# Third matrix product entirely by seven half products, with the order of all later instructions written anew

## The chip, the cores and the metric

One core of a Trainium2 chip runs the whole kernel. The metric is the device time of one execution in microseconds; a comparison uses the median over several runs. The profiled execution has a time of its own, given beside its span.

## The reference

Causal attention over q, k, v (2 batches, 12 heads, 448 rows, 64 per head), then a gated layer, then a hard-swish layer, all in float32:

```python
x = attention(q, k, v)                              # 896 x 768
x = ((1 / (1 + exp(-(x @ w_gate)))) * (x @ w_val)) @ w_out    # 768 -> 1536 -> 768
h = x @ w2_in                                       # 768 -> 2048
g = h * clip(h + 3, 0, 6) / 6
out = g @ w2_out                                    # 2048 -> 768
```

The weights come as float64 words and are turned into float32 on the chip.

## The kernel before

**Numbers.** Each factor is split into a high and a low part (`hi`, `lo`, both fp32r), and each product is three matrix products: hi·hi, hi·lo, lo·hi (`TERMS`). A split is either a ScalarE copy and a VectorE subtraction (`split`, `decode_b`), or two ScalarE copies (hi, and the negated source into lo) and a transfer on POOL's queue that adds the source to lo (`dma_split`, L186).

**Units.** The weights are cut into units of 128 x 768. A unit is loaded by SP into one of three `raw` slots, and decoded by one ScalarE scaling (`scale`) and four VectorE operations (`shift`, `clamp`, `join`, `sign`; `decode_a`, L208). `w_dec` (L699) decodes the next unit of the stream and loads the one three places on, which may start when the `sign` of the slot's old unit is through; `w_parts` (L710) splits units that are used plainly.

**Products.** Behind attention there are four matrix products: first (x with w_gate and w_val, units g0.. and v0..), second (with w_out, units o0.0.., giving y), third (y with w2_in, 16 units i0 to i15), last (with w2_out). All but the last have 448 columns in a matrix instruction, the two halves (b = 0, 1) of the 896 rows. A *plain block* (`halves`, L234) is 36 instructions for one unit: 6 slices, 3 terms, 2 halves. A *pair* (class `Pairs`, L718) does two units together by Strassen's way with seven half products P1 to P7 of 9 instructions each, 63 in all. It needs sums and differences of the pair's weights (`w_sums`: four VectorE operations into S) split into factors g1 to g4, of the moving side the four forms T1 to T4 beside three plain blocks of it (B11, B21, B22), and additions of the products (the copies C11, C12, C22 by ScalarE, `add`s by VectorE).

**Order of a pair run** (`run`, L845): P1, P2 of pair p, P4 of pair p-1, P6 of p, P3 of p-1, P5 and P7 of p. Pair 0 has no P4 and P3 of an earlier pair between. In the first product pairs are called a0 to a9, in the third c0, c1, ...

**The third product before.** Units i0 to i3 go by plain blocks (`NPL3` = 4; loop at L1177), i4 to i15 by six pairs. Between the plain blocks the code prepares pair 0's factors and the forms T2 and T1 (`y_split`, L1110: three splits each of 448 columns, one for each y column pair); T3 and T4 follow within pair 0. The forms are made out of combinations (t3, y12, y11, t4) of y columns o and o + 3, in the loop of the second product (L1081); so the last third of each form needs the last column, o = 5.

**Homes.** Tiles reuse each other's memory by tag. Pair 0's g1 and g4 of the third product lie in r11, its sums S in r10. r11 held the first factor of the second product's slices 10 and 11, r01 that of slices 1 and 2.

**Order of the instructions.** Everything behind attention is recorded by `Later` (L46, which is therefore the line of all of it in the profile) and then given out by hand: all instructions of ScalarE, VectorE, POOL and SP have a number (ScalarE from 0, then VectorE, POOL, SP, each in the order of the program text); `ORDER` lists them in the order in which they are given out, and `AHEAD` says how many TensorE instructions are given out ahead of each. TensorE keeps the order of the program. On each engine the instructions run in the order of the table; waits between engines come from the data.

Of the kernel before, what the change touches and what calls it, by code (L numbers as in the profile page):

```python
# [8 lines left out]
F32 = mybir.dt.float32  # L9
# [61 lines left out]
def kernel(  # L71
# [12 lines left out]
    nc = tc.nc  # L84
# [36 lines left out]
    NPL3 = 4  # L121
# [139 lines left out]
    with tc.manual_schedule():  # L261
# [456 lines left out]
        class Pairs:  # L718
# [93 lines left out]
            def P6(self, p):  # L812
                self.product(self.banks[p][0], self.grp[p, 2], 0, "T2", False)
# [267 lines left out]
        for o in range(KD):  # L1081
# [4 lines left out]
            for s in range(2):  # L1086
# [14 lines left out]
                if 2 * o + s in (4, 6):  # L1101
                    w_dec()
# [55 lines left out]
        def g1_at3(p):  # L1158
            if p == 0:
                late["g"] = acts.tile([P, 3, UN], F32R, tag="r11", name="g")  # L1160
                return late["g"][:, 0], late["g"][:, 1]
            return tiles_at(6 if (third.n - p) % 2 == 0 else 0, 2)
# [14 lines left out]
        for f in range(NPL3):  # L1177
            ph = acc()
            halves(ph, at3 + f, y_of, 0, True, True)
            if f == NPL3 - 1:  # L1180
                w_dec()
            plain3(f, ph)
            if f == 0:
                third.w_g1(0)
                third.w_sums(0)
                third.w_g4(0)
                w_dec()
                w_parts()
                y_split("T2")
            elif f == 1:  # L1190
                third.w_g2(0)
                y_split("T1")
                w_dec()
            elif f == 2:
                third.w_g3(0)
# [32 lines left out]
        third.turn = (2, 5, 4, 0, 1, 6, 7, 3)  # L1228
# [7 lines left out]
        double_banks(third.ps, [0, 3, 2, 1, 1, 0, 3, 2])  # L1236
# [3 lines left out]
        for c in range(2):  # L1240
# [101 lines left out]
        )  # L1342
        AHEAD = (
# [70 lines left out]
```

## Time and profile before

| | |
|---|---|
| median of three runs | 580.68 us (579.01 to 583.23) |
| profiled execution | 580.51 us, span 578.7 us |
| TensorE, matrix instructions | 569.0 us busy (98% of the span), 3236 instructions |
| VectorE | 458.0 us busy (79%) |
| ScalarE | 332.7 us busy (57%) |
| POOL | 88.9 us busy (15%) |

The stages follow each other: attention to about 95 us, with the first plain blocks of the first product begun in it; the first product to 262 us; the second to 350; the third to 458; the last to 574.5, then its last copy and transfer. A matrix instruction's busy time in the profile is longer than its share of the stream, since they are pipelined; the pace is read from starts.

### The profile page before, as it was taken

The numbers are of one execution on the slowest core, as the hardware profiler recorded it, in microseconds if no ns is written. First come the engines' busy times: TensorE is split into PE (matmuls) and PEld (weight loads), VectorE is DVE, ScalarE is ACT, GpSimd is POOL, SyncE is SP. The second block draws the span as 40 slices with busy tenths as digits, with TensorE's granted clock in tenths as the row PEclk, the third lists the DMA queues.
The fourth block names the chain that finished last, engine by engine and source line by source line (L and its number), as shares of the span: only waits on it lengthen the run. The fifth ranks groups of instructions, "written<-read, shape, count | busy, mean of one in ns | idle before, by whom it ended". The sixth has DMA issues, their size and how long they took to land.

```text
span 578.7 us, 8632 instructions
## 1 busy us (share of the span) xinstructions
PE 569.0 (98%) x3236; PEld 502.5 (87%) x3237; DVE 458.0 (79%) x692; ACT 332.7 (57%) x630; POOL 88.9 (15%) x146
## 2 busy tenths in 40 slices
PE   9999999998999999999999999999999999999997
PEld 5666556897999999999999999999999999999996
DVE  4789998878889989999876678987897999967301
ACT  5888887294665576595432335677777864233101
POOL 2645645030111111100000000021221000000000
PEclk9999999999999999999999999999999999999999
DMA  8756640477856777662461624398897134437002
GB/s 157 169 139 144 145 138 16 149 145 185 210 145 164 196 188 218 169 159 68 149 197 57 201 73 128 90 215 194 207 241 180 55 110 117 153 90 228 0 1 95
DMA packets 86921, 82.21 MB, mean 142 GB/s; under 512 B 35680, under 2 KB 77408, under 8 KB 86880
## 3 DMA queue, kind: packets, MB, share of 16 engines
q1 hardware_dynamic: 79904, 64.27, 37.9%
q0 software_dynamic: 6048, 17.17, 16.3%
q8 instruction: 25, 0.41, 0.3%
q10 hardware_dynamic: 928, 0.23, 0.2%
q14 instruction: 16, 0.13, 0.1%
HBM read 61.73 MB, written 2.75 MB: 111 GB/s over the span
## 4 chain that ended last, share of the span: by engine, by line
PE 82%; DVE 9%; ACT 3%; DMA 3%; issue 1%; SPq 0%; POOL 0%; ACTq 0%; DVEq 0%
PE m L46 40%; PE w L46 34%; PE pav L441 2%; PE s L367 2%; PE pt L421 2%; ACT pr L391 1%; DVE nm L379 1%; DMA raw<-in_moe_w_gate_dram 1%; DMA raw<-in_moe_w_val_dram 1%; DVE b L46 1%; DVE b L181 1%; PE tr L334 1%; DVE b L175 1%; DVE pth L431 1%; DVE tsum L280 1%
## 5 line engine op out<-in xcount | busy, mean ns | idle before, releaser
L46 PE MATMUL m<-hi,g 128*128 128x384 f32 x448 | 114.0, 334 | 0.0
L46 ACT ACTIVATE b<-raw 128x768 f32<-128x768 f32 x62 | 56.1, 907 | 53.5 <-DVE lo L46 23.2
L46 PE MATMUL w<-T,hi 128*128 128x448 f32 x288 | 82.4, 367 | 2.3 <-ACT raw L46 2.3
L46 PEld LDWEIGHTS m<-hi,g 128*128 128x128 f32 x448 | 80.9, 188 | 0.0
L46 PE MATMUL m<-lo,g 128*128 128x384 f32 x224 | 74.8, 334 | 0.0
L46 PE MATMUL m<-g,hi 128*128 128x448 f32 x288 | 70.2, 366 | 0.0
L46 PEld LDWEIGHTS w<-T,hi 128*128 128x128 f32 x288 | 54.0, 188 | 7.5 <-ACT raw L46 2.7
L46 DVE SCALAR_TENSOR_TENSOR b<-b,raw 128x768 int32<-128x768 int32 x62 | 58.9, 954 | 1.1
L46 DVE SCALAR_TENSOR_TENSOR b<-raw,b 128x768 int32<-128x768 int32 x62 | 58.8, 954 | 1.1
L46 PEld LDWEIGHTS m<-g,hi 128*128 128x128 f32 x288 | 54.0, 188 | 4.3
L46 ACT CAST hi<-b 128x768 fp32r<-128x768 f32 x32 | 26.7, 836 | 53.9 <-DVE b L46 40.8
L411 POOL TENSOR_SCALAR pr<-pr,rc 128x192 f32<-128x192 f32 (+3 forms) x96 | 48.7, 526 | 48.8 <-DVE rc L403 40.1
L46 PE MATMUL w<-T,lo 128*128 128x448 f32 x144 | 52.7, 366 | 0.0
L46 POOL DMA_DIRECT2D lo<-S x30 | 29.1, 985 | 135.1 <-ACT lo L46 116.0
L46 DVE TENSOR_SCALAR b<-b 128x768 f32<-128x768 f32 x62 | 34.4, 555 | 16.8 <-ACT b L46 16.7
L391 ACT ACTIVATE pr<-s,nm 128x192 f32<-128x192 f32 (+3 forms) x96 | 44.6, 477 | 4.7 <-DVE rc L403 2.5
L46 DVE TENSOR_SCALAR raw<-raw 128x768 int32<-128x768 int32 x62 | 33.9, 555 | 11.6 <-DMA raw<-in_moe_w_in_dram 5.6
L46 PEld LDWEIGHTS m<-lo,g 128*128 128x128 f32 x224 | 42.1, 188 | 0.0
L46 PE MATMUL m<-g,lo 128*128 128x448 f32 x144 | 40.9, 365 | 0.0
L46 PE MATMUL w<-x,g 128*128 128x448 f32 x180 | 38.1, 365 | 0.0
L46 DVE TENSOR_TENSOR lo<-b,hi 128x768 fp32r<-128x768 f32 x32 | 30.4, 951 | 8.0 <-ACT hi L46 7.9
L46 PEld LDWEIGHTS w<-x,g 128*128 128x128 f32 x180 | 33.8, 188 | 2.7
(128 smaller groups left out, 1078.6 us busy)
## 6 DMA issues: line engine op xcount, KB each, us to landing
raw<-in_moe_w_out_dram SPq DMA_DIRECT2D x28, 768.0 KB, 4.4
raw<-in_moe_w_in_dram SPq DMA_DIRECT2D x16, 768.0 KB, 4.8
lo<-S POOLq DMA_DIRECT2D x30, 384.0 KB, 4.5
raw<-in_moe_w_gate_dram SPq DMA_DIRECT2D x12, 768.0 KB, 5.3
raw<-in_moe_w_val_dram SPq DMA_DIRECT2D x12, 768.0 KB, 4.6
q<-in_q_dram SPq DMA_DIRECT2D x24, 112.0 KB, 3.7
g<-b POOLq DMA_DIRECT2D x7, 384.0 KB, 5.6
k<-in_k_dram SPq DMA_DIRECT2D x22, 112.0 KB, 3.7
```

The lines of the kernel that those rows point to most:

```text
L46: steps.append((name, lambda: fn(*args, **kw)))
L175: nc.vector.scalar_tensor_tensor(bi, bi, 3, words(u)[1], op0=ALU.logical_shift_left, op1=ALU.bitwise_or)
L181: nc.vector.scalar_tensor_tensor(bi, words(u)[0], -(2 ** 31), bi, op0=ALU.bitwise_and, op1=ALU.bitwise_or)
L280: op(r, a.bitcast(F32), b.bitcast(F32))
L334: nc.tensor.transpose(ps[:, c * CP : (c + 1) * CP], t[:, c].rearrange("p j d -> p (j d)"), identf[:CP, :CP],)
L367: nc.tensor.matmul(live["s", p, t][:, j], lhsT=live["qt", p][r, Q0[t] : Q0[t] + P], rhs=live["kt", p][r, : Q1[t]], start=False, stop=True, ...
L379: nc.vector.tensor_reduce(nm, live["s", p, t], axis=AX.X, op=ALU.max, negate=True)
L391: nc.scalar.activation(to if j else to[:, ::-1], ps[:, j].rearrange("p (c d) -> p c d", d=D), AF.Exp, bias=nm[:, j : j + 1], accum_out=sm[ ...
L411: nc.gpsimd.tensor_scalar(pr[:, j], pr[:, j], rc[:, j : j + 1], 1.0, op0=ALU.mult, op1=ALU.mult)
L421: nc.tensor.transpose(ps[:, o : o + P], live["pr", p, t].rearrange("p j n -> p (j n)")[:, c : c + P], identf,)
L431: nc.vector.tensor_copy(t[:, :m], ps[:, :m])
L441: nc.tensor.matmul(pav[r, Q0[i] :] if i else pav, lhsT=x[:, j] if i else x.rearrange("p j d -> p (j d)"), rhs=pt[g][:, off : off + w], sta ...
```

## The change

- `NPL3` is 0: units i0 to i15 go by eight pairs c0 to c7. The loop of plain blocks goes; what stood in it (pair 0's g1, sums, g4, g2, g3, forms T2 and T1) stands straight behind the second product in the text.
- Pair 0's g1 and g4 of the third product lie in r01 in place of r11.
- One matrix product of 64 columns, on pair 0's g2, is put ahead of pair 0's P6; its result is overwritten by P5.
- One early `w_dec` in the second product (at 2·o + s = 6) goes.
- The PSUM banks are taken in another turn.
- `ORDER` and `AHEAD` are worked out anew for the whole of the program behind attention, by a planner that was given longer transfers. There are 372 instructions of ScalarE (354 before), 546 of VectorE (532), 48 on POOL's queue (42) and 67 on SP's (67); TensorE has 2348 recorded matrix products (2365).

```diff
-    NPL3 = 4
+    NPL3 = 0
...
             def P6(self, p):
+                if self.ahead and p == 0:
+                    t = self.grp[p, 2][0].bitcast(F32)[:, :D]
+                    nc.tensor.matmul(
+                        self.banks[p][1][:D, :D], lhsT=t, rhs=t, start=True, stop=True
+                    )
                 self.product(self.banks[p][0], self.grp[p, 2], 0, "T2", False)
...
-                if 2 * o + s in (4, 6):
+                if 2 * o + s == 4:
                     w_dec()
                 w_dec()
                 w_parts()
...
-                late["g"] = acts.tile([P, 3, UN], F32R, tag="r11", name="g")
+                late["g"] = acts.tile([P, 3, UN], F32R, tag="r01", name="g")
...
-        for f in range(NPL3):
-            ph = acc()
-            halves(ph, at3 + f, y_of, 0, True, True)
-            if f == NPL3 - 1:
-                w_dec()
-            plain3(f, ph)
-            if f == 0:
-                third.w_g1(0)
-                third.w_sums(0)
-                third.w_g4(0)
-                w_dec()
-                w_parts()
-                y_split("T2")
-            elif f == 1:
-                third.w_g2(0)
-                y_split("T1")
-                w_dec()
-            elif f == 2:
-                third.w_g3(0)
+        third.w_g1(0)
+        third.w_sums(0)
+        third.w_g4(0)
+        w_parts()
+        y_split("T2")
+        third.w_g2(0)
+        y_split("T1")
+        third.w_g3(0)
...
-        third.turn = (2, 5, 4, 0, 1, 6, 7, 3)
+        third.turn = (4, 5, 2, 3, 0, 6, 7, 1)
...
-        double_banks(third.ps, [0, 3, 2, 1, 1, 0, 3, 2])
+        double_banks(third.ps, [2, 1, 0, 3, 3, 2, 1, 0])
...
```

The two tables differ nearly everywhere. Read back into names, two places of them matter below. (y4b1: second half of y column 4; `yc5 t3`: the combination t3 of columns 2 and 5; T2.2: last third of T2; `hi`, `lo`, `-lo`: the steps of a split; v2, g5: units.)

Order of the new table, start of the first product:

```
VectorE: t_op3, t_op4, a0 sum1, shift v2, a0 sum3, a0 sum2, clamp v2, t_op5, clamp v3, t_op6, shift v3, t_op7,
         join v3, join v2, xT4 lo, sign v2, shift g4, a0 sum4, plain1 mul, sign v3, a1 sum1 to sum4, a0 g4 lo,
         xT2 lo, plain3 mul, a1 g1 lo, a1 g4 lo, shift g5, clamp g4, join g4, sign g4
ScalarE: ... plain2 sigmoid, a1 g2 -lo, a1 g4 hi, a1 g3 -lo, a0 C11copy, scale g4, a0 C12copy, a1 g2 hi, scale g5
(before, VectorE: ... plain3 mul, shift g5, a1 sum4, a1 sum3, a1 g1 lo, a0 C11 add, clamp g4, a1 g4 lo, join g4)
```

Order of the new table, from the last y column but one to the end of pair 0:

```
VectorE: yc4 t3, y4b1 lo, sign i3, y2b0 lo, yc4 y12, yc4 y11, y3b0 lo, yc3 t4, c0 sum1 to sum3, c1 sum1, c0 sum4,
         T2.0 lo, T2.1 lo, y4b0 lo, c1 sum2, T1.1 lo, shift i5, yc4 t4, T1.0 lo, c1 sum3, c1 sum4, T3.0 lo, shift i4,
         yc5 t3, y5b0 lo, yc5 y12, yc5 y11, y5b1 lo, yc5 t4, T2.2 lo, T1.2 lo, T3.1 lo, T3.2 lo, T4.1 lo, T4.0 lo
ScalarE: ... c0 g3 -lo, T1.0 hi, T3.1 hi, T3.0 hi, c1 g1 -lo, T4.1 hi, y5b1 hi, y5b0 hi, c1 g1 hi, c0 C11copy,
         c1 g2 -lo, T2.2 hi, T1.2 hi, T4.0 hi, T3.2 hi, c0 g3 hi, c0 C12copy, scale i4
POOL:    transfers of c0 g1, c0 g2, c0 g3, c1 g1, c1 g2, c1 g3   (before: c0 g1, c0 g2, c1 g1, c0 g3, c1 g2, c1 g3)
```

## Rows read from the trace of the kernel before

**Rows 1.** Chain of waits in order of time: start us, us, what.
```profile
142.09 120.65 PE w L46 x594
262.73 117.19 PE m L46 x578
379.93 77.99 PE w L46 x378
457.92 116.50 PE m L46 x672
```

**Rows 2.** TensorE in order of time: start, us, operation [idle before, releaser].
```profile
142.09 0.67 PE L46 MATMUL w<-T,hi 128*128 128x448 f32 x2 [2.31 <-ACT raw L46]
```

**Rows 3.** TensorE in order of time, second and third product, columns as above.
```profile
262.66 0.33 PE L46 MATMUL m<-g 128*64 128x64 f32 x2
262.92 1.08 PE L46 MATMUL m<-g,hi 128*128 128x448 f32 x4
...
350.58 0.98 PE L46 MATMUL m<-y,hi 128*128 128x448 f32 x4
...
379.76 3.81 PE L46 MATMUL w<-y,g 128*128 128x448 f32 x18
...
387.47 0.39 PE L46 MATMUL w<-T,lo 128*128 128x448 f32 x1
387.70 0.57 PE L46 MATMUL w<-T,hi 128*128 128x448 f32 x2
...
388.94 3.88 PE L46 MATMUL w<-y,g 128*128 128x448 f32 x18
392.66 2.02 PE L46 MATMUL w<-T,g 128*128 128x448 f32 x9
```

**Rows 4.** Stretches: us, PE, PEld, DVE, ACT, POOL busy (x), clock, DMA share, GB/s.
```profile
132.20:142.10 9.90, 7.59 (x38) 6.49 (x36) 7.38 (x11) 3.88 (x7) 0.85 (x1) 1.00 0.93 230
350.70:379.90 29.20, 29.20 (x146) 27.05 (x145) 25.51 (x39) 17.33 (x27) 3.43 (x4) 1.00 0.44 109
379.90:457.90 78.00, 78.00 (x380) 70.88 (x379) 66.76 (x108) 58.50 (x88) 12.91 (x14) 1.00 0.80 192
```

**Rows 5.** POOL's queue in order of time: two transfers handed out (c1 g1, c0 g3).
```profile
376.85 0.84 POOL L46 DMA_DIRECT2D g<-b  x1 [5.41 <-ACT g L46]
377.39 1.19 POOL L46 DMA_DIRECT2D lo<-S  x1
```

**Rows 6.** SP, VectorE, ScalarE in order of time, ahead of the gap at 142.
```profile
131.33 0.37 SPq L46 DMA_DIRECT2D raw<-in_moe_w_gate_dram  x1
...
138.31 0.58 DVE L46 TENSOR_SCALAR raw<-raw 128x768 int32<-128x768 int32 x1 [0.83 <-DMA raw<-in_moe_w_gate_dram]
...
140.72 0.90 ACT L46 ACTIVATE b<-raw 128x768 f32<-128x768 f32 x1 [3.36 <-DVE g L46]
141.52 0.51 ACT L46 COPY raw<-w 128x448 f32<-128x448 f32 x1
```

**Rows 7.** Transfers, KB each, us to landing: 110 to 145 us, then 380 to 458.
```profile
lo<-S POOLq DMA_DIRECT2D x2, 384.0 KB, 10.0
...
lo<-S POOLq DMA_DIRECT2D x10, 384.0 KB, 4.3
```

**Rows 8.** Groups of instructions: engine, shapes, count | busy us, mean ns | idle before.
```profile
L46 DVE SCALAR_TENSOR_TENSOR b<-b,raw 128x768 int32<-128x768 int32 x62 | 58.9, 954 | 1.1
L46 DVE TENSOR_SCALAR raw<-raw 128x768 int32<-128x768 int32 x62 | 33.9, 555 | 11.6 <-DMA raw<-in_moe_w_in_dram 5.6 <-DMA raw<-in_moe_w_out_dram 4.4 <-DMA raw<-in_moe_w_gate_dram 1.5
L46 ACT ACTIVATE lo<-S 128x768 fp32r<-128x768 f32 x30 | 25.2, 843 | 2.7 <-PE w L46 1.5 <-DVE S L46 1.1
L46 DVE TENSOR_TENSOR S<-b 128x384 f32<-128x384 f32 x30 | 16.4, 552 | 0.5
L46 DVE TENSOR_TENSOR T<-yr,T 128x448 fp32r<-128x448 f32 x12 | 7.2, 616 | 0.0
L46 ACT CAST T<-yr 128x448 fp32r<-128x448 f32 x12 | 6.2, 568 | 0.0
```

195 rows, old and new, of tables (AHEAD, ORDER) are left out of this document.

## The prediction

> **What bounds the kernel now.** I read the chain of waits first, then TensorE in order of time, then the engines by stretch. From 142.09 us on the chain is TensorE alone: the first product's pairs, the second product and the four plain blocks in one piece, the third product's pairs, the last product [rows 1]. So behind 142 us two things move the time: the number and pace of matrix instructions, and gaps between them. TensorE's own listing shows one gap of any size, 2.31 us before 142.09 [rows 2].
>
> The pace has two values. In the plain blocks 144 instructions run from 350.58 to 379.76: 202.6 ns each. From 388.94 eighteen take 3.72 us: 206.7 ns each. The change sits at 387.47, where a matmul with a first factor that a transfer had made ("lo") starts 0.23 us ahead of its successor instead of 0.20 [rows 3]; the 77.99 us that the 378 pair instructions take [rows 1] say that the slow pace then held to the end of the pairs. The granted clock is 1.00, the 2.4 GHz level, in all these stretches [rows 4], so this is no change of clock.
>
> **The third product.** Before, it takes 379.76 − 350.58 = 29.18 us of plain blocks [rows 3] and 77.99 us of pairs [rows 1], 107.17 us. A plain block is 36 instructions for one unit, a pair 7 products of 9 = 63 for two. The change takes 4 × 36 = 144 away and puts 2 × 63 = 126 in; with the 378 that stay it is 504. At 202.6 ns that is 102.11 us, at 206.7 ns 104.18. The added 64-column product has a twin at the head of the second product, from 262.66 to 262.92: 0.26 us [rows 3]. So the stage takes 102.37 or 104.44 us, a gain of 4.80 or 2.73 us. I take the first. The late part at 387.47 is c0 g3's; its transfer was handed out at 377.39, 0.54 us behind c1 g1's [rows 5], which is used later. The new order on POOL hands out c0 g3 first. And the twin of the added product was followed by the 202.6 ns pace, as was the 2.31 us gap: a full stop gives the fast pace back. Both ends stay in the range.
>
> A page of the Trainium skill knows one pace only (TensorE: Matmul & The Clock Gate, Back-to-back issue gap): columns over 2.4 GHz plus 2.5 ns, 189.2 ns for 448 columns. By that rule the 18 instructions are worth 3.4 us and nothing comes back from the pace; the time would be 575.6 us. The trace has 202.6 and 206.7, and the sum goes by the trace.
>
> **The gap at 142 us.** TensorE waits for a ScalarE copy out of PSUM [rows 2], a0 C12copy. That copy took its turn at 141.52, behind the scaling of unit g4, which had waited 3.36 us for VectorE's a1 g1 lo; VectorE had been held by the shift of unit g5, whose load was issued at 131.33 and let it start at 138.31 [rows 6]. In the new order the shift of g5 stands behind a1 g1 lo and a1 g4 lo, so that load no longer holds them. I walked VectorE's new order from 110 us on, with lengths as in [rows 8] and the earlier loads landing as before: sign v2, which frees the slot for g5, ends near 125, six us ahead of the old issue; a1 g4 lo ends near 135; ScalarE then scales g4 and copies C12 by 138.5, its product having ended at 137.6; P7 is due at 139.5. The accumulating transfers need 10 us here [rows 7]; a0 g3's starts near 128, so it is in by 138 to 139. So the gap goes: −2.31 us. If it stays, 0.
>
> **The joint between second and third product.** The plain blocks were 29 us of cover, under which VectorE (25.5 us busy) and ScalarE (17.3) split T forms and made the first pair's factors [rows 4]. Without them TensorE goes from the end of the last y column (time zero here) to P1 and P2 of pair 0, which need columns that are long split, and y5b0; then P6 needs T2, whose last third comes out of that very column. Cover: P1 and P2, the small product, and P6 up to the first use of T2's last low part: 25 × 0.2026 + 0.26 = 5.3 us.
>
> VectorE ahead of zero: from yc4 t3, which can't start before 72 × 0.2026 = 14.6 us ahead, to shift i4 stand 14 operations on 448 columns, one sign, 8 sums and 2 shifts: 14 × 0.616 + 0.954 + 8 × 0.552 + 2 × 0.555 = 15.1 us [rows 8]. So full lengths, end to end, leave it free at +0.5. Then t3, y5b0 lo, y12, y11, y5b1 lo, t4, T2.2 lo: 7 × 0.616 = 4.3, ready at 4.8. ScalarE: y5b1, y5b0, c1 g1 hi, C11copy (not before P1's end, 1.9), c1 g2 −lo, T2.2 hi: 1.9 + 0.57 + 0.84 + 0.57 = 3.9 [rows 8], in time. T1's and T3's last thirds follow at 5.4 and 6.6, against uses at 7.2 and 8.8. The new home (r01) makes this possible: r01's old content is last read early in the last column, r11's at its very end, so pair 0's factor can be split ahead of zero. c0 g3's transfer starts near −2, c1 g1's near −0.5; they land 4.3 to 10.0 us later [rows 7], against uses at 8.0 and 9.8. By the rows, then, no wait, with half a us to spare. Above, the nearest row is the gap at the first product's own start, 2.31 us [rows 2]. I take 0.4, near the lower end.
>
> **Other engines.** VectorE gains 14 operations (per added pair 4 sums, a split, 3 adds, 3 hard-swish steps; less 4 low parts and 4 hard-swish steps of the plain blocks), ScalarE 18, POOL's queue 6 transfers of 384 KB. They lie under TensorE as long as a pair costs VectorE less than 63 × 0.2026 = 12.76 us. In the old pair stretch VectorE is busy 66.76 of 78.00 us for six pairs, 11.1 a pair, and POOL 12.91 us in all [rows 4]. The cover is thin, 1.6 us a pair; past it everything comes onto the path. The dropped w_dec moves a decode by one place: 0.
>
> **Sum.** Profiled 580.51 (span 578.7 and what lies around it): − 4.80 − 2.31 + 0.40 = 573.8. The median is 580.68, 0.17 above the profiled execution: 574.0 us.
>
> **Rivals.**
> *Slow pace.* A weight part that comes a little late again puts the third product on 206.7 ns: 2.07 us less gained, 576.0. For it: some 340 of the 378 old pair instructions ran so. Against: the new order of the transfers, and that nothing of the kind befell the first two products. The page named above comes near the same time.
> *The gap stays,* or one like it opens elsewhere: 576.3. For it: transfers of 10 us in that stretch, and an order that is new everywhere. Against: the walk has about 1 us to spare at each place.
> *The joint waits.* A VectorE that comes b us late to its first operation behind zero costs b − 1: 3 to 6 us late give 575.6 to 578.6. For it: 15.1 us of work in 14.6.
> *Slower: VectorE sets the pace of the pairs.* At full lengths a pair is 4 × 0.555 + 4 × 0.954 for two decodes, 4 × 0.552 sums, 0.552 split, 5 × 0.616 for adds and half hard-swishes, twice 0.616 for the whole one: 13.1 us, above 12.76 [rows 8]. With the y5 and T work left behind zero (14 × 0.616) the stage is 8 × 13.1 + 8.6 = 113.4 us in place of 102.4: 584.6 with no other wait at the joint. It decides as soon as VectorE has no idle time left in the pairs; 0.3 us more per pair takes it beyond 586.5. Against it: the 11.1 us measured a pair.
>
> **How the numbers follow.** A measurement of this kernel tells about 1% from no change: below 574.9 is faster, above 586.5 slower. Chances: forecast 0.45 (572.5 to 574.9); slow pace 0.21; a gap like the old one 0.12; joint 0.12; VectorE 0.10, of which 0.07 beyond 586.5. So faster 0.45, same 0.48, slower 0.07. The range takes in the forecast, both cases at 576 and most of the joint, 572.3 to 579.5, and leaves out VectorE's case and the joint's worst.
>
> **What would show it.** In the new trace: 504 pair instructions at 202.6 or 206.7 ns; no gap on TensorE at 139 to 142 us; behind the second product P1, P2, the small product and P6 with no idle time between; VectorE below 95% busy in the pairs. A wait at P6 on T, at P7 on a transferred "lo", or a new gap in the last product makes the prediction wrong.

## The result, and the profile after

The changed kernel takes 573.84 us (median of 8, 572.76 to 575.85), the kernel before 579.85 us (median of 8, 578.74 to 583.23): ratio 0.9899, interval 0.9873 to 0.9925. That is 1.0% faster, 6.0 us between the medians; the forecast was 574.0 us.

The chain of waits of the changed kernel, in order of time (start us, us, what), answers to [rows 1]:

```profile
105.19 5.77 PE m L240 x27
110.96 22.32 PE m L46 x108
133.28 127.75 PE w L46 x630
261.02 88.01 PE m L46 x434
349.03 102.60 PE w L46 x506
451.63 116.52 PE m L46 x672
```

In this execution TensorE is the chain from 105 us on without a break, and the third product is one piece of 102.60 us. The entry by VectorE, ScalarE and transfers, which ran up to 142 us before, is shorter, but not gone: this execution runs at the slow pace from 105.4 to 136.6 us and so hides what is left of it. In the second profiled execution (after_again), which has no slow pace there, the chain enters TensorE only at 136.50, at P6 of the first pair:

```profile
126.54 8.15 DMA lo<-S
...
135.19 0.84 ACT lo L46
136.04 0.43 ACT raw L46
136.50 124.30 PE w L46 x612
```

P6 waits there for the copy of C11 (136.04), which stands on ScalarE behind work that waited for an accumulating transfer of 8.15 us. Of the nine profiled executions with the changed order (experiments included) six start this P6 0.2 to 0.9 us late.

The joint and the pace in it, TensorE in order of time (answers to [rows 3]):

```profile
348.87 3.81 PE L46 MATMUL w<-y,g 128*128 128x448 f32 x18
352.61 0.33 PE L46 MATMUL w<-hi 128*64 128x64 f32 x2
352.87 0.67 PE L46 MATMUL w<-T,hi 128*128 128x448 f32 x2
```

P1 and P2 take 3.74 us to the next start (18 x 0.2027 = 3.65 and a bump of 0.09 at the small product; a bump is an instruction that starts a little late, with no idle mark in the profile), the small product 0.26 us, then P6: no wait. From here to 451.47 the pace is 202.7 ns. VectorE in the same place, and by stretch (columns as in [rows 4]):

```profile
353.40 3.29 DVE L46 TENSOR_TENSOR T<-yr,T 128x448 fp32r<-128x448 f32 x6
```

```profile
349.00:451.60 102.60, 102.60 (x508) 94.79 (x507) 93.69 (x150) 79.50 (x122) 18.27 (x21) 1.00 0.82 191
```

The first of the six is T2.2 lo: with 0.62 us of length it ends at 354.02, 5.15 us behind the end of the second product. The first that needs it is a weight load of P6:

```profile
354.19 0.19 PEld L46 LDWEIGHTS w<-T,hi 128*128 128x128 f32 x1
```

So 0.2 us were to spare. VectorE is busy 93.69 of 102.60 us, 91%.

Where the 6.87 us between the two profiled spans (578.73 and 571.86) lie, from the starts of TensorE's stages; beside them the same for one more profiled execution of each (before_again, after_again, below). The slow pace lies elsewhere in each: before has it from 387 us to the end of the third product, before_again from 105 to 140 us, after from 105 to 137 us, after_again nowhere:

| stretch | before | after | difference | before_again | after_again | difference |
|---|---|---|---|---|---|---|
| start to the head of the second product | 262.66 | 260.95 | -1.71 | 262.64 | 260.74 | -1.90 |
| second product, small product included | 87.92 | 87.92 | 0.00 | 87.92 | 87.91 | -0.01 |
| third product | 107.18 | 102.60 | -4.58 | 106.06 | 102.60 | -3.46 |
| last product and end | 120.97 | 120.39 | -0.58 | 121.05 | 120.38 | -0.67 |
| span | 578.73 | 571.86 | -6.87 | 577.67 | 571.63 | -6.04 |

### The profile page after: what moved, and what is told of

The parts are those of the page before. It is cut to its first block, busy times and chain, and to the rows that moved or that the text cites. A ratio compares the mean times of both kernels' runs of the same rounds, so it can differ in the third digit from the quotient of the medians.

```text
span 571.9 us, 8667 instructions
## 1 busy us (share of the span) xinstructions
PE 565.2 (99%) x3220; PEld 500.2 (87%) x3221; DVE 462.9 (81%) x706; ACT 344.5 (60%) x648; POOL 92.5 (16%) x152
## 4 chain that ended last, share of the span: by engine, by line
PE 90%; DVE 6%; ACT 2%; issue 1%; POOL 0%; DVEq 0%
PE w L46 40%; PE m L46 40%; PE pav L441 2%; PE pt L421 2%; PE s L367 2%; ACT pr L391 1%; DVE nm L379 1%; PE tr L334 1%; PE pt L533 1%; PE m L240 1%; DVE tsum L280 1%; DVE b L175 1%; DVE pth L431 1%; DVE raw L167 1%; DVE b L181 1%
## 5 line engine op out<-in xcount | busy, mean ns | idle before, releaser
L46 PE MATMUL w<-T,hi 128*128 128x448 f32 x324 | 92.1, 366 | 0.0
L46 PEld LDWEIGHTS w<-T,hi 128*128 128x128 f32 x324 | 60.8, 188 | 4.9
L46 PE MATMUL w<-T,lo 128*128 128x448 f32 x162 | 59.2, 365 | 0.0
L46 POOL DMA_DIRECT2D lo<-S x34 | 30.4, 898 | 152.9 <-ACT lo L46 98.2
L46 ACT CAST hi<-b 128x768 fp32r<-128x768 f32 x28 | 23.5, 838 | 38.4 <-DVE b L46 27.2
L46 DVE TENSOR_TENSOR lo<-b,hi 128x768 fp32r<-128x768 f32 x28 | 26.6, 954 | 16.5 <-ACT hi L46 16.2
L46 ACT CAST g<-b 128x384 fp32r<-128x384 f32 (+1 forms) x36 | 23.9, 675 | 20.8 <-PE w L46 11.2
```

The lines of the kernel that those rows point to most:

```text
L46: steps.append((name, lambda: fn(*args, **kw)))
```

## The experiments

Each kernel ran beside the kernel before on the same chip. In the diffs of the order, only what moves is shown, in names.

**The gap at 142 us: the order, or the late load?** Two kernels cross the two suspects.

before_shift_later:

```diff
 VectorE, kernel before:
-  plain3 mul, shift g5, a1 sum4, a1 sum3, a1 g1 lo, a0 C11 add
+  plain3 mul, a1 sum4, a1 sum3, a1 g1 lo, shift g5, a0 C11 add
```

> The kernel before, with one place of its order changed: VectorE's shift of unit g5 is moved from behind the last plain block's product to behind a1 g1 lo. The load of g5 stays late (issued near 131.3 us). Theory A (the order was the cause: a late load held VectorE, ScalarE's scaling and with it the copy of C12): the gap of 2.31 us ahead of the first pair's P7 goes, below 0.3 us, and the time falls by about 2 us. Theory B (the late load is the cause and stays one): the gap stays, or one of at least 1 us opens behind it, at the next pair; time within 0.5 us of the kernel before.

Measured: median 578.03 us, ratio to the kernel before 0.9964 (0.9945 to 0.9982), 2.1 us between the medians. TensorE in order of time:

```profile
141.40 0.67 PE L46 MATMUL w<-T,hi 128*128 128x448 f32 x2 [0.54 <-ACT raw L46]
```

The gap shrinks, but it does not vanish. This execution ran at the slow pace up to the gap, as before_again did (below), where the gap is 1.63 us; so 1.63 to 0.54 is the fair comparison, not 2.31 [rows 2] to 0.54. Counted from the start of the first plain block to that of P7, the time goes from 47.04 (before_again) to 45.95 us, 1.1 us less; with the whole new order (after_again) it is 44.97. So moving the shift was about half of what the new order gave, and neither theory's figure is met. The 2.1 us between the medians are too much for it: eight of the sixteen times of the kernel before lie in an upper group above 580.7 us, and none of the ten here does; the lower groups are 1.2 us apart. What is left is not the late load: the shift now runs behind a1 g1 lo and holds nobody up, and ScalarE's scaling of g4, just ahead of the copy of C12, still waits for VectorE's a1 g1 lo:

```profile
139.98 0.94 ACT L46 ACTIVATE b<-raw 128x768 f32<-128x768 f32 x1 [1.96 <-DVE g L46]
```

after_shift_earlier:

```diff
 VectorE, changed kernel:
-  plain3 mul, a1 g1 lo, a1 g4 lo, shift g5
+  plain3 mul, shift g5, a1 g1 lo, a1 g4 lo
 SP: load g5 given out right behind sign v2 (where it ran already)
```

> The changed kernel, with the shift of unit g5 put back ahead of a1 g1 lo on VectorE, its load as early as in the changed kernel (issued near 125.4 us, landed at 132.75). Theory A (the order alone): VectorE is held by the load again and a gap of 1 to 2.5 us opens ahead of the first pair's P7. Theory B (the earlier load alone makes the order harmless): the shift finds its unit landed, no gap, time as the changed kernel within 0.5 us.

Measured: median 573.85 us, ratio to before 0.9892 (0.9858 to 0.9926). VectorE in order of time shows the shift (second line) with no wait for its load:

```profile
133.24 1.09 DVE L46 TENSOR_TENSOR raw<-m,raw 128x896 f32<-128x896 f32 x1 [1.23 <-PE m L46]
134.25 0.55 DVE L46 TENSOR_SCALAR raw<-raw 128x768 int32<-128x768 int32 x1
```

TensorE has no gap there, and the copy of C12 ends at 139.29, 1.1 us ahead of P7. So theory B: with the load issued at 125.2 the place of the shift no longer matters in the changed kernel. That the earlier load alone would have done it in the kernel before is not shown: the rest of the order differs too (a1's sums run from 128.0 to 130.1 us here, from 134.0 to 139.8 before), and no run moves the load alone.

**The joint: what the new home is worth.** after_r11:

```diff
-                late["g"] = acts.tile([P, 3, UN], F32R, tag="r01", name="g")
+                late["g"] = acts.tile([P, 3, UN], F32R, tag="r11", name="g")
```

> The changed kernel, with pair 0's g1 and g4 of the third product back in r11, everything else as changed. r11's old content is read to the end of the second product. Theory: the home is what lets the joint go without a wait; in r11 the split can only start at that end, so P1 waits for two ScalarE steps, the hand-out on POOL (1 us) and a transfer of 4 to 5 us: 6 to 9 us without TensorE work behind the second product, and time 6 to 9 us longer (579 to 583). Rival: the order of the table hides it, since other work can go first: below 2 us.

Measured: median 583.07 us, ratio to before 1.0061 (1.0035 to 1.0087): slower than the kernel before, 9.2 us above the changed kernel's median (8.5 above that of after_again, which ran beside it). TensorE in order of time, ScalarE in the same place, and two stretches:

```profile
355.75 6.63 PE L46 MATMUL w<-y,g 128*128 128x448 f32 x18 [6.16 <-ACT g L46]
```

```profile
349.62 0.51 ACT L46 CAST g<-b 128x384 fp32r<-128x384 f32 x1 [14.05 <-PE m L46]
```

```profile
349.00:355.80 6.80, 0.64 (x4) 0.26 (x3) 2.63 (x5) 6.18 (x11) 1.70 (x2) 0.93 0.32 58
355.80:361.50 5.70, 5.70 (x15) 5.12 (x16) 5.28 (x11) 5.70 (x11) 1.70 (x2) 0.50 0.95 172
```

ScalarE stands 14.05 us before pair 0's g4 because r11 is read to the end of the second product, and everything behind it on ScalarE stands too. TensorE waits 6.16 us, as long as the theory has it, but not for the transfer: that one lands at 355.03, and the wait ends with ScalarE's hi part of pair 0's g1 (354.86 to 355.69), the tenth step counted from the one above. So the price belongs to the home together with an order that was made for r01; an order made for r11 was not tried. A second price was not expected: behind the wait the granted clock is 0.50 (the 1.2 GHz level) for 5.7 us, eighteen instructions take 6.6 us in place of 3.7. That is 2.8 us more, and with the wait about 9. The profiled execution (585.24 us) lies above the median, since the rest of its third product ran at the slow pace. Behind the gaps of 1.6 and 2.3 us at 142 us the clock stayed at 1.00.

**The form without the order.** Both kernels with the tables left out, so that every engine runs in the order of the program text:

```diff
-        ORDER = (
...
+        ORDER = ()
+        AHEAD = ()
```

> The kernel before with the hand-written order left out: all engines run in the order of the program text. Only the base for the next kernel. Both theories: slower than 581 us, some 590 to 640, with gaps on TensorE wherever ScalarE's or VectorE's next step waits in front of one that TensorE needs.

> The changed kernel with the hand-written order left out. Theory: the 18 instructions are a gain only with an order that gets the forms and pair 0's factors ready ahead of the joint; in program order these all stand behind the last y column, so a wait of 5 us or more opens behind the second product, and this kernel is not faster than the kernel before in program order (0 to 10 us slower). Rival: the gain lies in the form of the product alone; 3 us or more faster than the kernel before in program order.

Measured: 580.57 us for the kernel before, 592.18 us for the changed one. The waits of TensorE in the changed kernel from the second product to the start of the third, then the only one of the kernel before between 380 and 392 us, at its first pairs:

```profile
329.52 1.08 PE L46 MATMUL m<-g,hi 128*128 128x448 f32 x4 [1.51 <-ACT hi L46]
346.06 1.08 PE L46 MATMUL m<-g,hi 128*128 128x448 f32 x4 [1.50 <-ACT hi L46]
357.17 1.11 PE L46 MATMUL w<-y,g 128*128 128x448 f32 x2 [3.35 <-ACT g L46]
362.39 5.46 PE L46 MATMUL w<-y,g 128*128 128x448 f32 x16 [4.11 <-DMA g<-b]
374.77 1.48 PE L46 MATMUL w<-y,g 128*128 128x448 f32 x6 [0.39 <-DMA g<-b]
```

```profile
390.18 2.09 PE L46 MATMUL w<-y,g 128*128 128x448 f32 x9 [1.48 <-DMA g<-b]
```

Three readings, each from one execution of each kernel. The kernel before hardly needs its table: 580.57 us without, 578.7 to 583.2 with; my "590 to 640" for it was wrong. In program order it has no gap at 142 us at all, P7 of the first pair starts at 139.52:

```profile
139.52 0.56 PE L46 MATMUL w<-T,hi 128*128 128x448 f32 x2
```

and from TensorE's end to the end of the span it takes 3.71 us, as the changed kernel does, against 4.33 with its table. So the gap and the longer end were made by the old table, and what the new one gains at these two places is their repair, not the change of the third product. Last, the 18 instructions saved are turned into a loss of 11.6 us, more than the 10 of the theory. The waits at the start of the third product (3.35 and 4.11 us, with half the clock behind them) are the missing cover: nothing gets pair 0's factors ready ahead, and the order has to replace what the plain blocks gave. But 3.0 us of the loss are the two waits inside the second product, for the split of a decoded unit, which the kernel before does not have in program order; the w_dec that the change drops there may be their cause, and no run separates it.

**How thick VectorE's cover is.** Additions of 128 columns on a tile that nobody uses, behind the C11 addition of each of c1 to c7 (n = 4 or 12):

```diff
             others[k]()
+            if k in self.extra:
+                for _ in range(n):
+                    self.nc.vector.tensor_add(self.pad, self.pad, self.pad)
```

> The changed kernel with 4 additions of 128 columns on VectorE (on a tile of their own, used by nobody) added in each of the pairs c1 to c7, behind the addition of C11; some 0.2 us each, 0.8 us a pair. Theory: VectorE has about 1.1 us of idle time a pair in the third product (93.7 of 102.6 us busy) and TensorE takes no notice: no gap above 0.3 us, third product within 1 us. Rival: VectorE already sets the pace there: 0.8 us a pair, 5 to 6 us longer.

> The changed kernel with 12 such additions in each of the pairs c1 to c7, some 2.4 us a pair. Theory: past the 1.1 us of idle time all comes onto the path: 7 x 1.3, about 9 us longer (the third product 108 to 113 us, gaps on TensorE in the pairs, or in the last product's first part). Rival: what VectorE does ahead of its use (decodes, sums) is so far ahead that most of it is taken up: below 4 us longer.

One addition takes 0.29 us, so 28 are 8.1 us and 84 are 24.5 us. Measured: 577.14 and 595.38 us; the spans are 575.2 and 593.6 against 571.6 of after_again, so 3.6 and 22.0 us longer. With four a pair TensorE waits in the last pairs:

```profile
439.50 2.09 PE L46 MATMUL w<-T,g 128*128 128x448 f32 x9 [0.86 <-ACT g2r L46]
449.72 0.67 PE L46 MATMUL w<-y,hi 128*128 128x448 f32 x2 [0.83 <-ACT g2r L46]
452.93 2.09 PE L46 MATMUL w<-T,g 128*128 128x448 f32 x9 [1.12 <-DVE g2r L46]
```

The theory falls: 1.16 us a pair were added in place of 0.8 (an addition was longer than I took it for), which is hardly more than the 1.1 us of idle time a pair, and still 3.6 of 8.1 us came through, all in the third product. The idle 8.9 us of the stage take up 4.5. TensorE's first wait comes only at 439 us: the lateness adds up over the pairs until the lead that VectorE had is used up. With twelve a pair 22.0 of 24.5 come through; two of the waits, 2.94 and 5.46 us, brought stretches at half the granted clock again, so this number holds more than VectorE's own time:

```profile
438.81 0.68 PE L46 MATMUL w<-y,hi 128*128 128x448 f32 x2 [2.94 <-DVE g2r L46]
```

```profile
439.90:442.60 2.70, 2.70 (x9) 2.40 (x8) 2.67 (x5) 2.40 (x5) 0.00 (x0) 0.50 1.07 248
```

So VectorE does not set the pace of the changed kernel, but it is some 4 us, in 102, from doing so, for additions at this one place of the pair.

**The pace: 202.7 or 206.7 ns.** after_again and before_again are the two kernels unchanged.

> The changed kernel once more, unchanged, to see whether the place of TensorE's slow pace (206.7 ns an instruction in place of 202.7) is fixed by the program. Theory: it is not; the profiled execution has another stretch at the slow pace than 105 to 136 us, and times differ by 2 us from one execution to the next, as a stage at the one or the other pace does. Rival: the slow stretch is tied to the program's place 105 to 136 us and shows there again.

> The kernel before once more, unchanged. Theory: the gap ahead of the first pair's P7 is the program's and shows again (2 to 2.6 us at about 140 us); the stretch at 206.7 ns from 387.5 us on is not and lies elsewhere or is absent, the time then being 579 us without one and 581 us or more with one. Rival: both show again.

Measured: after_again has a median of 574.58 us (573.41 to 576.06, four times; ratio to before 0.9910, 0.9875 to 0.9944). Its profiled execution took 573.41 us and has no stretch at the slow pace at all behind 105 us; the first profile of the same kernel (573.63 us) has it from 105.4 to 136.6 us. before_again 579.44 us: the gap at 142 shows again, the slow pace lies at 105 to 140 us and not in the third product, though a bump at the same weight part shows again at 387:

```profile
142.06 0.67 PE L46 MATMUL w<-T,hi 128*128 128x448 f32 x2 [1.63 <-ACT raw L46]
```

```profile
387.04 0.57 PE L46 MATMUL w<-T,hi 128*128 128x448 f32 x2
387.61 0.47 PE L46 MATMUL w<-T,lo 128*128 128x448 f32 x1
387.91 0.56 PE L46 MATMUL w<-T,hi 128*128 128x448 f32 x2
```

So the gap is the program's and the pace is not. The gap is 1.63 us here, below the 2 to 2.6 expected, because TensorE came to it later at the slow pace, while P7 could start at the same time (142.06 and 142.09). Whole stages at the slow pace would explain the spread of the times, which lie in two groups 2 us apart for either kernel (group against group the changed kernel is 5.3 to 5.4 us faster). Of the upper group only three executions of the changed kernel or its variants were profiled, those of after_shift_earlier, after_no_small and after_r11, and each has a long slow stretch. In after_shift_earlier's (575.93 us, against 573.2 to 574.1 in its three others) the slow pace holds from 105.3 to 263.0 us, which costs 157.7 x (1 - 202.7 / 206.7) = 3.1 us, and ends at the small product at the head of the second product.

after_no_small takes the small product ahead of P6 away (its result is overwritten anyway):

```diff
             def P6(self, p):
-                if self.ahead and p == 0:
-                    t = self.grp[p, 2][0].bitcast(F32)[:, :D]
-                    nc.tensor.matmul(
-                        self.banks[p][1][:D, :D], lhsT=t, rhs=t, start=True, stop=True
-                    )
```

> The changed kernel without the 64-column product ahead of pair 0's P6; its order of all other instructions is kept. By the sum it costs 0.26 us: P6 then follows P2 at the usual pace (0.20 us) and the third product takes 102.2 to 102.4 us in place of 102.6 when its pace is 202.7 ns. Rival: P6 has to wait there anyway, for T2 or its weights, so that the same 0.1 to 0.3 us come back as a wait. If a stop draws the pace anew, the third product can also run at 206.7 ns more often (2 us more) than with it.

Measured: median 575.94 us (573.13 to 577.33; five of six times above 575.3), ratio to before 0.9922 (0.9894 to 0.9950). Its third product takes 104.30 us in the profiled execution and is at the slow pace from 355 us to its end. TensorE's weight loads, then its matmuls in order of time:

```profile
354.47 0.19 PEld L46 LDWEIGHTS w<-T,hi 128*128 128x128 f32 x1 [0.34 <-DVE T L46]
```

```profile
354.14 0.81 PE L46 MATMUL w<-T,hi 128*128 128x448 f32 x2
354.79 0.37 PE L46 MATMUL w<-T,lo 128*128 128x448 f32 x1
```

P6 now runs into T2's last third, which is late by a third of a us, and the slow pace begins at that bump. In this profile the product that I had priced at 0.26 us is worth more than it costs: without it the stage is 1.70 us longer. Five of six times above 575.3 us, against five of twelve with it, are too few to say how often that happens, so the 2.1 us between the medians are not shown to be its worth. Whether it helps by keeping P6 off the late T2 or by a stop of its own, this run cannot separate.

after_small_first adds one more such product, ahead of the first product's third plain block, in the changed kernel:

```diff
                 ps = acc()
+                if j == 2:
+                    w = split_t[at1[f, v]][0].bitcast(F32)[:, :D]
+                    nc.tensor.matmul(ps[:D, 0, :D], lhsT=w, rhs=w, start=True, stop=True)
                 halves(ps, at1[f, v], x_of, 0, True, True)
```

> The changed kernel with one more 64-column product, ahead of the first product's third plain block (0.26 us). Theory: TensorE's pace is drawn at a stop; at the end of attention the slow one (206.7 ns) is drawn often and then holds for 30 to 157 us, behind a 64-column product nearly always the fast one; so behind 118 us the profile shows 202.7 ns whatever it shows ahead, the times of 575.5 us and more become rare, and the median is 572.8 to 574.0. Rival: the slow pace comes and goes by itself; the times lie in the same two groups as those of the changed kernel, plus 0.26 us.

> The changed kernel with the additional 64-column product ahead of the first product's third plain block, once more, for more times. Theory (the product draws TensorE's pace anew, mostly the fast one): at most 1 or 2 in 6 times in the upper group (575.3 us and more), against 5 in 12 for the changed kernel so far; median 573.2 to 573.9. Rival (no influence): 2 or 3 in 6 in the upper group, median 573.9 to 575.5.

Measured: medians 573.51 (0.9894, 0.9861 to 0.9926) and 573.44 us (0.9889, 0.9861 to 0.9917). 2 of 12 times lie above 575.3 us, against 5 of 12 of the changed kernel. TensorE of the second run, at the place of the added product:

```profile
116.79 0.57 PE L46 MATMUL m<-x,hi 128*128 128x448 f32 x2
117.20 0.37 PE L46 MATMUL m<-x,lo 128*128 128x448 f32 x1
117.41 0.57 PE L46 MATMUL m<-x,hi 128*128 128x448 f32 x2
117.82 0.37 PE L46 MATMUL m<-x,lo 128*128 128x448 f32 x1
118.12 0.33 PE L46 MATMUL m<-hi 128*64 128x64 f32 x2
...
119.70 0.97 PE L46 MATMUL m<-x,hi 128*128 128x448 f32 x4
120.51 0.57 PE L46 MATMUL m<-x,lo 128*128 128x448 f32 x2
120.92 0.97 PE L46 MATMUL m<-x,hi 128*128 128x448 f32 x4
```

Ahead of it three instructions take 0.62 us (116.79 to 117.41, 206.7 ns each), behind it six take 1.22 us (119.70 to 120.92, 203 ns each): the slow pace ends there. In the first run it had not set in. 2 and 5 of 12 are too few to call the times different; the place where the pace turns is shown, in one execution.

## Why the prediction was right, point by point

**The third product.** Forecast 107.17 to 102.37 us. Measured 107.18 to 102.60: the counts, the 202.7 ns and the small product's 0.26 us are right. But 4.58 us is not the change's own worth. The kernel before ran its pairs at the slow pace in the profiled execution I started from, and in before_again it did not: 106.06 us. The change's own part is 3.46 us, the 18 instructions less the small product (18 x 0.2027 - 0.26 = 3.39). The rest belongs to that one execution. That the new order of transfers would keep the pace was the wrong reason; the pace turns up in other places from one execution to the next. Nor did the trace before show that a full stop gives the fast pace back: ahead of the 2.31 us gap and of the twin of the small product the pace was fast already. Later runs show both: before_again's slow stretch ends at the gap, and after_r11 turns slow behind a wait of 6.16 us and a small product. The base was about as much above the kernel's usual time as the term was above the change's usual worth (580.51 us, against 579.44 of before_again and 579.85 in the median), so the sum came out right by luck. The slow-pace rival did not occur here in the third product, but it is what after_no_small does.

**The page's constant pace.** By the rule that I set beside this (the Trainium skill, TensorE: Matmul & The Clock Gate, Back-to-back issue gap), 18 instructions were worth 3.4 us. Less the small product that is 3.1 us, near the 3.46 measured between two executions whose third product ran at the fast pace; its 189.2 ns for 448 columns is not what the trace shows, 202.7. I was wrong that the page knows one pace only: this section calls that formula the gap of a single isolated matmul and gives a shorter spacing for streams of weight loads and matmuls, 131 ns at 512 columns, which the 202.7 ns at 448 columns here do not bear out either.

**The gap at 142 us.** The chain was read rightly, but its share was not. The late load held VectorE for 0.83 us [rows 6]; with the 0.5 us of the shift itself that is 1.3 of the 2.31, and moving the shift alone gave 1.1. The rest lay in other parts of the order. The walk put a1 g4 lo's end near 135, C12 at 138.5 and no gap. In the trace VectorE's a1 g4 lo ended at 138.2, late by three us for a wait for a transfer that the walk had not in it (2.29 us), while ScalarE scaled g4 at 136.51 and copied C12 at 138.86:

```profile
137.63 0.56 DVE L46 TENSOR_TENSOR g<-b,g 128x384 fp32r<-128x384 f32 x1 [2.29 <-DMA lo<-S]
```

```profile
136.51 0.89 ACT L46 ACTIVATE b<-raw 128x768 f32<-128x768 f32 x1
138.86 0.54 ACT L46 COPY raw<-w 128x448 f32<-128x448 f32 x1 [1.46 <-PE w L46]
```

C12 waited for its product, as forecast, and not for the scaling. The term was mis-sized: to the head of the second product the gain is 1.71 us (1.90 in the other two executions) in place of 2.31. Two things stand behind that. The first plain block starts up to 0.4 us later (95.32 in place of 94.90, 95.29 against 95.02). And the walk left out C11: P6 needs its copy, which ends near 136.5 behind the 8 us transfer shown above, so P7, two products behind P6, can start at 140.3 (after_again) and not at 139.5. "About 1 us to spare at each place" did not hold there.

**The joint.** Forecast by rows: T2.2 lo at 4.8 us against 5.3, no wait; I added 0.4 for safety. Measured 5.15 against 5.32 (the weight load that needs it) and no wait: the 0.4 was the wrong part of the step, the walk was right to 0.4 us. after_r11 shows that this order needs the home, and after_no_small that without the small product's 0.26 us nothing is to spare.

**Other engines.** Forecast: they lie under TensorE. Right, but my 1.6 us a pair was too thick: 8.9 us of idle time over eight pairs are 1.1, and the additions show that 1.16 us a pair is more than the cover holds.

**The end.** Priced at nothing, and 0.58 to 0.67 us came from there. Output transfers stood in line on SP behind the wait for one copy (out 3) and were handed out six in a row; in the new table the ones that are ready go first. SP's queue at the end of the kernel before, then of the changed one:

```profile
573.01 2.80 SPq L46 DMA_DIRECT2D out_dram<-osb  x6
```

```profile
564.67 4.50 SPq L46 DMA_DIRECT2D out_dram<-osb  x5
```

TensorE ends at 574.41 and 568.14. The row of six begins 1.4 us ahead of that end and reaches 1.4 us behind it, the row of five 3.5 ahead and 1.0 behind. From TensorE's end to the end of the span it is 4.33 us before and 3.72 after. I had read the new table only at its first product and at the joint. Against the forecast the start gained 0.60 us too little and the third product 0.22 (4.58 in place of 4.80); the end gained 0.58 that was not in the sum, and the 0.40 for the joint was not needed. These errors, of up to 0.6 us each, cancel to 0.16: the nearness of the sum is luck around a right core.

## What to carry to other kernels

A block of work that is dropped for its length may have been the cover of what comes next: price it by the first use behind it, with every operation of the busiest engine between, and find out what memory has to be free for that work to start early (here a home that is free some 54 instructions, 11 us, earlier was worth 9 us, with the order left as it was). Measure the base more than once before a gain is read out of a pace: two profiled executions of one kernel differed by 1.1 us in the very stage that was to be changed. Compare a gap between executions in which the engine that waits came to it at the same pace. And look at the last hand-outs of a new order, where half a us is to be had without any engine being faster.

## What the runs showed of the hardware that was not expected

TensorE's stream of weight load and matmul of 448 columns has two paces at the same granted clock of 1.00: 202.7 and 206.7 ns. The pace changes mostly at small bumps and at waits, and the slow one then held for up to 158 us. Where the plain blocks start behind attention's last products (105 us, with no idle time between) six of fourteen profiled executions ran slow, behind a 64-column product one of twenty-five. In 21 of these 25 the pace was fast ahead of it too, in two the granted clock was at its lower level shortly before; the two slow stretches that met such a product ended there. What in the chip sets it stays open.

The granted clock stayed at 1.00 behind stops of 1.6 to 2.3 us at 142 us and fell to 0.50 behind one of 6.2 us in after_r11, for 5.7 us, and behind those of 2.94 and 5.46 us in after_vector_12. That the clock is halved behind idle time and given back with work is what the Trainium skill says (TensorE: Matmul & The Clock Gate, What's actually happening), and the trace agrees: it made after_r11's wait of 6.2 us cost 9.
